# Transposing attention weights in 64-token halves, in turn from upper and lower rows into two banks

## The chip, the cores and the metric

One NeuronCore of a Trainium2 chip runs the whole program; the other cores are idle. The metric is device time in microseconds (us) of one execution, lower is better. The kernel before takes 581.49 us, the median of two executions (581.31 and 581.68).

## What is computed

Attention with a sliding window and sinks, followed by two feed-forward layers of two matrix products each, all in fp32:

```
scores = q @ k.T / sqrt(64)             # 2 batches, 8 heads, 768 tokens, head size 64
keep   = (column < n_sink) | (0 <= row - column < window)     # n_sink 4, window 128
a      = softmax(where(keep, scores, -1e9))
x      = (a @ v), heads side by side                          # 1536 tokens x 512
h = x @ w_in;  x = (h * clip(h + 3, 0, 6) / 6) @ w_out        # 512 -> 2048 -> 512
h = x @ w_in2; out = (h * sigmoid(1.702 * h)) @ w_out2        # 512 -> 2048 -> 512
```

## The kernel before

**Tiles.** There are 12 tiles of 128 tokens (`NTILE`). A tile's four pairs of heads are handled in two calls of `duo` (line 1122), so 24 duos of two pairs, four heads, each. One duo is: the scores on TensorE (PE), 24 small matmuls on 64x64 quarters of the array (L1152); for each of the four heads a masking with the row minimum on VectorE (DVE, L1167) and an exponential on ScalarE (ACT, L1175) into a tile `pexp` of 128 tokens by 196 keys, zero padded to 256; the inverse of the sums (DVE, L1183 and L1184); the scaling of `pexp` on DVE (L1194) or ACT (L1192); the transposes on PE (L1203), called "turns" here; and the copies of the transposed P from PSUM to the SBUF ring `pts` (ACT as L442, DVE as L444). After two duos `tile_values` (line 1215) multiplies P with V: 24 matmuls on 64 columns of the array (L1226, L1234). The result goes to SBUF as a high and a low part, `xy` (ACT L442, DVE L1253).

**Turns.** A turn takes one pair of heads: four transposes of 128x128, two heads by two chunks of keys, fill one PSUM bank of 512 columns, and one copy empties it into one `pts` tile. The transposed operand is the one that is loaded into the array (PEld), the identity is the one that is streamed.

**Feed-forward layers.** They run over blocks of 512 tokens and 16 slices of 128 hidden units: an "up" group is three matmuls of 128x512 per 128 inputs (L932), a "down" group three of 128x512 (L980), each on the whole array, with operands split in a high and a low part. The second layer of two of the three blocks is done later in another form (L616, L732). Weights are unpacked by DVE and ACT (L472 to L500).

**What sets the order.** Nothing is ordered by hand. `Plan` collects operations with costs per engine, dependences, buffers and due times, and `issue` emits them in the order of a greedy list schedule: each engine then runs its own list strictly in that order. So a change of costs, buffers or limits reorders the whole part in which attention and feed-forward work are mixed. `limit` (line 1295) decides which kind of work may take one of the eight PSUM banks: "s" scores, "t" turns, "v" values, "h" up, "y" down. The first block needs the first four tiles, so PE's list begins with attention alone (called the ramp here) and goes on with attention and feed-forward groups mixed until the twelfth tile; after it only feed-forward work is left.

## Time and profile before

| | us |
|---|---|
| median of two executions | 581.49 |
| the profiled execution | 582.17 |
| its span, first to last instruction | 580.4 |
| PE busy | 563.6 (97%) |
| DVE busy | 458.6 (79%) |
| ACT busy | 387.0 (67%) |
| POOL busy | 54.2 (9%) |

The profiled execution is 0.68 us above the median. Of its 582.17 us, 1.8 lie outside the span. Busy times of PE are modelled from starts, since matmuls overlap; pace is read from the distance of starts. PEld is the load of the array's stationary operand, which runs beside PE's matmuls. Most matmuls of plain fp32 data appear as two records each, the transposes as one.

### The profile page before, as it was taken

The numbers are of one execution on the slowest core, as the hardware profiler recorded it, in microseconds if no ns is written. First come the engines' busy times: TensorE is split into PE (matmuls) and PEld (weight loads), VectorE is DVE, ScalarE is ACT, GpSimd is POOL, SyncE is SP. The second block draws the span as 40 slices with busy tenths as digits, with TensorE's granted clock in tenths as the row PEclk, the third lists the DMA queues.
The fourth block names the chain that finished last, engine by engine and source line by source line (L and its number), as shares of the span: only waits on it lengthen the run. The fifth ranks groups of instructions, "written<-read, shape, count | busy, mean of one in ns | idle before, by whom it ended". The sixth has DMA issues, their size and how long they took to land.

```text
span 580.4 us, 11424 instructions
## 1 busy us (share of the span) xinstructions
PE 563.6 (97%) x4482; PEld 497.5 (86%) x4482; DVE 458.6 (79%) x958; ACT 387.0 (67%) x796; POOL 54.2 (9%) x62
## 2 busy tenths in 40 slices
PE   6889999999999999999999999999999999999996
PEld 6777887888878888888888888888888888999996
DVE  6699999999987666469999999984466665667784
ACT  6787768766755665456655678454478788768762
POOL 0000000000000000000000000000003344765000
PEclk8898999999999999999999999999999999999999
DMA  8973564234442000000444440420034567999512
GB/s 259 374 228 114 176 209 165 67 121 136 177 153 75 1 2 0 1 1 1 166 175 167 146 145 2 145 73 1 0 81 76 81 96 144 168 184 198 101 37 79
DMA packets 23468, 65.65 MB, mean 113 GB/s; under 512 B 2480, under 2 KB 10672, under 8 KB 19312
## 3 DMA queue, kind: packets, MB, share of 16 engines
q1 hardware_dynamic: 13360, 51.22, 26.4%
q0 software_dynamic: 10048, 13.63, 14.9%
q8 instruction: 37, 0.61, 0.4%
q14 instruction: 23, 0.19, 0.1%
HBM read 47.02 MB, written 3.15 MB: 86 GB/s over the span
## 4 chain that ended last, share of the span: by engine, by line
PE 79%; DVE 10%; ACT 4%; DMA 3%; issue 1%; DVEq 0%; SPq 0%; ACTq 0%
PE bank L932 24%; PE bank L980 23%; PE bank L732 13%; PE bank L616 13%; DMA stage<-in_w_dram 3%; PE bank L1203 2%; ACT pexp L1175 2%; DVE wf L500 2%; PE bank L1152 2%; DVE wf L493 1%; PE bank L1226 1%; PE bank L1234 1%; DVE pexp L1167 1%; DVE wg L565 1%; DVE wg L550 1%
## 5 line engine op out<-in xcount | busy, mean ns | idle before, releaser
L980 PE MATMUL bank<-wg 128*128 128x512 f32 x768 | 189.5, 381 | 0.8 <-ACT wg L442 0.8
L980 PEld LDWEIGHTS bank<-wg 128*128 128x128 f32 x768 | 143.7, 189 | 22.1 <-ACT wg L442 1.2
L932 PE MATMUL bank<-xy,w0h 128*128 128x512 f32 x512 | 155.9, 386 | 2.1 <-ACT xy L442 1.4
L932 PEld LDWEIGHTS bank<-xy,w0h 128*128 128x128 f32 x512 | 95.9, 190 | 16.4 <-issue 1.7
L932 PE MATMUL bank<-xy,w0l 128*128 128x512 f32 x256 | 97.7, 382 | 0.1
L680 POOL DMA_DIRECT2D wf<-wf x24 | 29.0, 1288 | 467.3 <-ACT wf L661 432.0
L442 ACT CAST wg<-wf 128x512 fp32r<-128x512 f32 x78 | 48.3, 620 | 30.8 <-PE bank L980 23.3
L944 ACT ACTIVATE u<-bank,three 128x512 f32<-128x512 f32 x48 | 32.8, 684 | 40.1 <-PE bank L932 39.9
L550 DVE TENSOR_TENSOR w0l<-wf,w0h 128x512 fp32r<-128x512 f32 x72 | 49.3, 685 | 12.2 <-ACT w0h L442 12.2
L932 PEld LDWEIGHTS bank<-xy,w0l 128*128 128x128 f32 x256 | 48.8, 191 | 7.5 <-DVE w0l L550 0.5
L550 DVE TENSOR_TENSOR wg<-wf,wg 128x512 fp32r<-128x512 f32 x64 | 43.9, 686 | 13.5 <-ACT wg L442 13.5
L949 DVE SCALAR_TENSOR_TENSOR u<-u,bank 128x512 f32<-128x512 f32 x48 | 32.7, 682 | 23.5 <-ACT u L944 23.5
L472 ACT ACTIVATE wf<-stage 128x1024 f32<-128x1024 f32 x32 | 38.0, 1187 | 18.5 <-DMA stage<-in_w_dram 17.7
L1175 ACT ACTIVATE pexp<-pexp,nb 128x196 f32<-128x196 f32 x96 | 42.9, 449 | 9.0 <-DVE nb L1167 8.8
L565 DVE TENSOR_TENSOR wg<-u,wg 128x512 fp32r<-128x512 f32 x64 | 43.9, 687 | 1.3 <-ACT wg L442 0.2
L442 ACT CAST wg<-u 128x512 fp32r<-128x512 f32 x59 | 36.6, 621 | 12.3 <-DVE u L949 12.3
L493 DVE SCALAR_TENSOR_TENSOR wf<-stage,wf 128x1024 int32<-128x1024 int32 x32 | 39.1, 1221 | 0.3
L500 DVE SCALAR_TENSOR_TENSOR wf<-stage,wf 128x1024 int32<-128x1024 int32 x32 | 39.0, 1220 | 0.3
L576 ACT ACTIVATE u<-bank 128x512 f32<-128x512 f32 x32 | 19.1, 596 | 29.0 <-PE bank L932 21.9
L616 PE MATMUL bank<-xy,w0h 128*128 128x512 f32 x128 | 38.1, 379 | 0.0
L442 ACT CAST w0h<-wf 128x512 fp32r<-128x512 f32 x60 | 36.7, 611 | 0.8 <-PE bank L616 0.5
L1203 PE MATMUL bank<-ident,pexp 128*128 128x128 f32 x192 | 29.3, 296 | 4.2 <-DVE pexp L1194 2.4
(188 smaller groups left out, 994.8 us busy)
## 6 DMA issues: line engine op xcount, KB each, us to landing
stage<-in_w_dram SPq DMA_DIRECT2D x32, 1024.0 KB, 4.9
wf<-wf POOLq DMA_DIRECT2D x24, 256.0 KB, 3.8
wf<-in_kq_dram SPq DMA_DIRECT2D x8, 520.0 KB, 11.3
vc<-in_vc_dram SPq DMA_DIRECT2D x12, 320.0 KB, 5.8
vb<-in_v_dram SPq DMA_DIRECT2D x10, 256.0 KB, 6.6
kept<-in_kq_dram SPq DMA_DIRECT2D x4, 520.0 KB, 11.0
aside<-wf SPq DMA_DIRECT2D x4, 256.0 KB, 3.0
aside<-wf POOLq DMA_DIRECT2D x4, 256.0 KB, 5.1
```

Source lines behind the costliest of these rows:

```text
L442: eng.copy(out, in_)
L472: lambda e: e.activation(w.tile.bitcast(F32), top.bitcast(F32), AF.Abs),
L493: lambda e: e.scalar_tensor_tensor(out=w.tile, in0=top, scalar=-0x40000000, in1=w.tile, op0=ALU.bitwise_and, op1=ALU.bitwise_or),
L500: lambda e: e.scalar_tensor_tensor(out=w.tile, in0=low, scalar=29, in1=w.tile, op0=ALU.logical_shift_right, op1=ALU.bitwise_or),
L550: lambda e: e.tensor_tensor(out=lo.tile[at], in0=of(), in1=hi.tile[at].bitcast(F32), op=ALU.subtract),
L565: lambda e: e.tensor_tensor(out=gl.tile, in0=parted(u.tile), in1=gh.tile.bitcast(F32), op=ALU.subtract),
L616: e.matmul(bank.tile, l, woven(r), start=(begin and j == 0 and k == 0), stop=(j == 1 and k == 2), skip_group_check=True,)
L732: e.matmul(to, l, woven(t), start=(begin and n == 0 and m == 0 and e4 % share == 0), stop=(n == pairs - 1 and m == 2), skip_group_check=True,)
L932: e.matmul(h.tile[:, :n], w, woven(x), start=(c == 0 and k == 0), stop=(c == NC - 1 and k == 2))
L980: e.matmul(yb.tile, l, woven(r), start=(begin and k == 0), stop=(end is not None and k == 2))
L1175: lambda e, n=n: e.activation(pes[n].tile[:, :W], pes[n].tile[:, :W], AF.Exp, bias=nbs[n].tile, scale=-1.0, accum_out=z.tile[:, n : n + 1],),
L1203: e.transpose(pt.tile[:, n * P : (n + 1) * P], pes[2 * a + j].tile[:, x * P : (x + 1) * P], ident)
```

## The change

P is transposed in halves of 64 tokens. A turn still takes one pair of heads, but its four transposes become eight: for each 128x128 piece first the upper 64 rows into one bank, then the lower 64 rows into a second bank. Both turns of a duo fill the same two banks (the second joins with `adds`), and only then two copies run, one per bank, each for both pairs of heads. The ring `pts` has 3 tiles of twice the size in place of 6. The planner's cost of a turn goes from 440 to 250, and `limit` keeps two banks free for turns ("spared") where up and down groups, and scores, would take them. The values read the same data from the larger tile.

```diff
@@ -52,7 +52,7 @@
 NU = 3
 NG = 2
 PX = 8
-NPT = 6
+NPT = 3
 
 APART = 8
 
@@ -1089,7 +1089,7 @@
 
     def plan_attention(plan, pool, due):
 
-        sizes = {"nb": (8, [P, 1], F32), "z": (3, [P, 4], F32), "pts": (NPT, [P, 4, P], F32)}
+        sizes = {"nb": (8, [P, 1], F32), "z": (3, [P, 4], F32), "pts": (NPT, [P, 8, P], F32)}
         for cls, (n, shape, dt) in sizes.items():
             plan.ring(cls, n, lambda k, cls=cls, shape=shape, dt=dt: pool.tile(shape, dt, name=cls, tag=f"{cls}{k}"))
         kept = [pool.tile([P, KQ], F32, name="kept", tag=f"kept{j}") for j in range(KEPT)]
@@ -1194,23 +1194,35 @@
                         e.tensor_scalar_mul(x, x, r)
 
                 plan.op([("DVE", 232), ("ACT", 350)], scale, when, reads=[z], writes=[pes[n]])
+            pt, pb = [Buf(cls="bank", kind="t") for _ in range(2)], Buf(cls="pts")
             for a in range(2):
-                pt, pb = Buf(cls="bank", kind="t"), Buf(cls="pts")
-
-                def turn(e, a=a, pt=pt):
+
+                def turn(e, a=a):
                     for n in range(4):
                         j, x = divmod(n, 2)
-                        e.transpose(
-                            pt.tile[:, n * P : (n + 1) * P], pes[2 * a + j].tile[:, x * P : (x + 1) * P], ident
-                        )
-
-                plan.op([("PE", 440)], turn, when, reads=pes[2 * a : 2 * a + 2], writes=[pt], chain="turn")
-                plan.op(
-                    [("ACT", 478), ("DVE", 602)],
-                    lambda e, pt=pt, pb=pb: copy(e, pb.tile, pt.tile.rearrange("p (n t) -> p n t", t=P)),
-                    when, reads=[pt], writes=[pb],
-                )
-                pts.append(pb)
+                        o = (4 * a + n) * HALF
+                        for c in range(2):
+                            rows = slice(c * HALF, (c + 1) * HALF)
+                            e.transpose(
+                                pt[c].tile[:, o : o + HALF], pes[2 * a + j].tile[rows, x * P : (x + 1) * P],
+                                ident[rows, rows],
+                            )
+
+                plan.op(
+                    [("PE", 250)], turn, when, reads=pes[2 * a : 2 * a + 2], chain="turn",
+                    **(dict(adds=pt) if a else dict(writes=pt)),
+                )
+            for c in range(2):
+
+                def take(e, c=c):
+                    at = pb.tile[:, :, c * HALF : (c + 1) * HALF]
+                    copy(e, at, pt[c].tile.rearrange("p (n t) -> p n t", t=HALF))
+
+                plan.op(
+                    [("ACT", 478), ("DVE", 602)], take, when, reads=[pt[c]],
+                    **(dict(adds=[pb]) if c else dict(writes=[pb])),
+                )
+            pts.append(pb)
 
         def tile_values(T, pts):
             i = tok[T][1]
@@ -1221,7 +1233,7 @@
 
             def values(e):
                 for hp in range(NPAIR):
-                    p = pts[hp].tile
+                    p = pts[hp // 2].tile[:, hp % 2 * 4 : hp % 2 * 4 + 4, :]
                     for j in range(2):
                         e.matmul(
                             av.tile[j * D : (j + 1) * D, hp * P : (hp + 1) * P],
@@ -1300,22 +1312,24 @@
                 used = [x.kind for x in slots if x is not None and (x.left or x in o.new)]
                 free = len(slots) - len(used)
                 h, v, t = (used.count(x) for x in "hvt")
+                spared = t or free > 2 or not plan.left["t"]
                 if b.kind == "h":
-                    return h < (H_BANKS if plan.left["s"] == 0 else 2 if "y" not in used else 1)
+                    return h < (H_BANKS if plan.left["s"] == 0 else 2 if "y" not in used else 1) and spared
                 if b.kind == "q":
                     return h + used.count("q") < (4 if "y" in used else 6)
                 if b.kind == "s":
                     mine = o.new.index(b)
                     if mine == 0 and used.count("s") > (0 if "y" in used else 2):
                         return False
-                    return free > (1 - mine if v or t else 2 - mine)
+                    return free > (1 if t else 2 if v else 3) - mine
                 if b.kind == "v":
                     return v == 0 or free > 2
                 if b.kind == "y":
-                    return used.count("s") < 4
+                    return used.count("s") < 4 and spared
                 if b.kind == "t":
 
-                    return t + sum(1 for x in plan.slots["pts"] if x is not None and x.left) < NPT
+                    mine = o.new.index(b)
+                    return mine or t // 2 + sum(1 for x in plan.slots["pts"] if x is not None and x.left) < NPT
                 return True
 
             plan.limit = limit
```

What the planner makes of it is seen in each engine's list. In PE's list, where the first up groups (L932) have begun, the kernel before has these rows: turns (L1203) of the fifth tile, its scores (L1152), twelve matmuls of down groups (L980), the last turns and the first rows of the values (L1226).

```order
L1203 MATMUL bank<-ident,pexp 128x128 x4
L932 MATMUL bank<-xy,w0h 128x512 x2
L932 MATMUL bank<-xy,w0l 128x512
L1203 MATMUL bank<-ident,pexp 128x128 x4
L1152 MATMUL bank<-wf 64x64 x8
L1152 MATMUL bank<-wf 64x68 x4
L1152 MATMUL bank<-wf 64x64 x8
L1152 MATMUL bank<-wf 64x68 x4
L980 MATMUL bank<-wg 128x512 x12
L1203 MATMUL bank<-ident,pexp 128x128 x8
L980 MATMUL bank<-wg 128x512 x3
L1226 MATMUL bank<-pts,vb_64 64x128 x2
```

The changed kernel has these at the same place; L1206 are its turns, eight transposes of 128x64 per pair of heads, L1238 and L1246 its values.

```order
L1206 MATMUL bank<-ident,pexp 128x64 x8
L932 MATMUL bank<-xy,w0h 128x512 x2
L932 MATMUL bank<-xy,w0l 128x512
L1206 MATMUL bank<-ident,pexp 128x64 x24
L1152 MATMUL bank<-wf 64x64 x8
L1152 MATMUL bank<-wf 64x68 x4
L1152 MATMUL bank<-wf 64x64 x8
L1152 MATMUL bank<-wf 64x68 x4
L1238 MATMUL bank<-pts,vb_64 64x128 x2
L1246 MATMUL bank<-pts,vc_66 64x64 x2
```

The last two turns moved up to the second, and the down groups moved behind the values, so turns, scores and values now stand next to each other.

Further on in PE's list, at the sixth tile, the kernel before has two turns between down groups and scores, and two between scores and down groups:

```order
L980 MATMUL bank<-wg 128x512 x12
L1203 MATMUL bank<-ident,pexp 128x128 x8
L1152 MATMUL bank<-wf 64x64 x8
L1152 MATMUL bank<-wf 64x68 x4
L1152 MATMUL bank<-wf 64x64 x8
L1152 MATMUL bank<-wf 64x68 x4
L1203 MATMUL bank<-ident,pexp 128x128 x8
L980 MATMUL bank<-wg 128x512 x6
```

The changed kernel at the seventh tile, where its pattern is plain:

```order
L980 MATMUL bank<-wg 128x512 x3
L1206 MATMUL bank<-ident,pexp 128x64 x16
L932 MATMUL bank<-xy,w0h 128x512 x2
L932 MATMUL bank<-xy,w0l 128x512
L932 MATMUL bank<-xy,w0h 128x512 x2
L932 MATMUL bank<-xy,w0l 128x512
L980 MATMUL bank<-wg 128x512 x9
L1206 MATMUL bank<-ident,pexp 128x64 x16
L980 MATMUL bank<-wg 128x512 x3
```

The two turns of a duo now mostly stand together, with groups on the whole array on both sides.

On ACT, ahead of the copy of the fourth tile's result (`xy`), for which the first up group waits, the kernel before has from the third tile's copy on:

```order
L442 CAST xy<-bank 128x4x128
L1192 ACTIVATE pexp<-pexp,z 128x196 x2
L1175 ACTIVATE pexp,z<-pexp,nb 128x196
L442 CAST w0h<-wf 128x512
L442 COPY pts<-bank 128x512
L1192 ACTIVATE pexp<-pexp,z 128x196 x2
L442 COPY pts<-bank 128x512
L442 CAST wg<-wf 128x2x256
L442 COPY pts<-bank 128x512
L1175 ACTIVATE pexp,z<-pexp,nb 128x196
L442 CAST xy<-bank 128x4x128
```

and the changed kernel:

```order
L442 CAST xy<-bank 128x4x128
L472 ACTIVATE wf<-stage_61 128x1024
L1192 ACTIVATE pexp<-pexp,z 128x196
L442 COPY pts<-bank 128x8x64
L442 CAST wg<-wf 128x2x256
L442 COPY pts<-bank 128x8x64 x3
L1175 ACTIVATE pexp,z<-pexp,nb 128x196 x3
L472 ACTIVATE wf<-stage_60 128x1024
L442 CAST xy<-bank 128x4x128
```

Four copies of P, three exponentials and two unpackings stand between the two `xy` copies now, where three copies, two exponentials and none stood before.

## Rows read from the trace of the kernel before

**Rows 1.** The page: granted TensorE clock in 40 slices of 14.5 us, in tenths.
```profile
PEclk8898999999999999999999999999999999999999
```

**Rows 2.** Stretches: from:to, length, busy time (and instructions) of each engine, clock, DMA share, GB/s.
```profile
5.00:43.10 38.10, 30.50 (x738) 26.50 (x738) 31.98 (x136) 30.68 (x103) 0.00 (x0) 0.87 0.91 306
...
50.00:80.00 30.00, 30.00 (x361) 25.76 (x360) 29.69 (x67) 20.04 (x45) 0.00 (x0) 1.00 0.44 143
80.00:210.00 130.00, 128.39 (x1337) 109.08 (x1337) 114.94 (x287) 88.91 (x212) 0.00 (x0) 1.00 0.33 111
```

**Rows 3.** Waits of PE from 50 to 210 us: total, times, longest.
```profile
PE bank L980 <- ACT wg L442: 0.8, 1, 0.8
PE bank L1203 <- ACT pts L442: 0.6, 1, 0.6
```

**Rows 4.** Timeline of PE: start, time, line, shapes, records (mixed part, full clock).
```profile
103.51 0.81 PE L980 MATMUL bank<-wg 128*128 128x512 f32 x3
104.16 0.60 PE L1203 MATMUL bank<-ident,pexp 128*128 128x128 f32 x4
104.52 0.89 PE L980 MATMUL bank<-wg 128*128 128x512 f32 x3
```

**Rows 5.** Timeline of PE in the ramp: turns between values and scores.
```profile
18.43 0.66 PE L1203 MATMUL bank<-ident,pexp 128*128 128x128 f32 x4
19.02 0.93 PE L1152 MATMUL bank<-wf 64*64 64x64 f32 x48
...
21.68 1.09 PE L1203 MATMUL bank<-ident,pexp 128*128 128x128 f32 x8
22.70 0.93 PE L1152 MATMUL bank<-wf 64*64 64x64 f32 x48
```

**Rows 6.** Timeline of PE: from the whole array to scores and back.
```profile
98.35 0.38 PE L932 MATMUL bank<-xy,w0l 128*128 128x512 f32 x1
98.66 0.93 PE L1152 MATMUL bank<-wf 64*64 64x64 f32 x48
99.52 0.48 PE L932 MATMUL bank<-xy,w0h 128*128 128x512 f32 x1
```

**Rows 7.** Timeline of PE inside scores: 24 records lie between these two starts.
```profile
111.81 0.29 PE L1152 MATMUL bank<-wf,kept 64*64 64x64 f32 x8
...
112.16 0.29 PE L1152 MATMUL bank<-wf,kept 64*64 64x64 f32 x8
```

**Rows 8.** Groups of loads (PEld) from 50 to 210 us: busy us, mean ns of one, idle.
```profile
L980 PEld LDWEIGHTS bank<-wg 128*128 128x128 f32 x258 | 47.5, 189 | 8.4 <-ACT wg L442 1.2 <-DVE wg L565 0.4 <-DVE wg L550 0.2
...
L1203 PEld LDWEIGHTS bank<-ident,pexp 128*128 128x128 f32 x128 | 14.8, 140 | 3.2 <-ACT pts L442 1.0 <-issue 0.2 <-DVE pexp L1194 0.2
...
L1152 PEld LDWEIGHTS bank<-kept 64*64 64x64 f32 x336 | 6.1, 134 | 2.0 <-issue 2.0
```

**Rows 9.** Timeline of loads: the first two loads of turns after values.
```profile
18.43 0.20 PEld L1203 LDWEIGHTS bank<-ident,pexp 128*128 128x128 f32 x2
```

**Rows 10.** The chain that ended last, pieces in the ramp: start, us, what.
```profile
13.60 1.44 PE bank L1203 x6
...
25.36 2.02 issue
...
28.90 2.76 PE bank L1203 x12
```

**Rows 11.** Groups of ACT in the ramp (5 to 43.1 us): busy us, mean ns of one, idle.
```profile
L1175 ACT ACTIVATE pexp<-pexp,nb 128x196 f32<-128x196 f32 x33 | 14.7, 449 | 3.4 <-DVE nb L1167 3.4
L442 ACT COPY pts<-bank 128x512 f32<-128x512 f32 x13 | 7.5, 579 | 1.8 <-PE bank L1203 1.8
...
L442 ACT CAST xy<-bank 128x512 fp32r<-128x512 f32 x4 | 2.3, 580 | 2.1 <-PE bank L1234 2.1
L472 ACT ACTIVATE wf<-stage 128x1024 f32<-128x1024 f32 x2 | 2.3, 1141 | 0.0
...
L442 ACT CAST w0h<-wf 128x512 fp32r<-128x512 f32 x2 | 1.2, 612 | 0.1
```

## The prediction

> **What bounds the kernel now.** I read the stretches first. From 50 to 210 us, where attention and feed-forward groups are mixed, PE is busy for 158.4 of 160 us [rows 2], and only two waits of it are named, 1.4 us together [rows 3]. DVE has 144.6 of the 160, in the first 30 us nearly all. So PE's list sets the end there, DVE stands close behind, and what PE saves or loses up to 210 us goes to the end one to one, since after it the same feed-forward groups follow in both kernels. In the ramp, 5 to 43.1 us, no engine is full: PE 30.5, DVE 32.0, ACT 30.7 of 38.1 us [rows 2]. There the chain of waits shows what ends last: it runs through PE with turns in it (1.44 us for six, 2.76 us for twelve transposes), and through a stop of 2.02 us that nothing shown released [rows 10]. The granted clock is below nine tenths of full in the first, second and fourth slice of 14.5 us, and at nine tenths or more in all others [rows 1].
>
> **The turns themselves.** A block of four transposes lasts 0.59 us from its start to the scores' start, one of eight 1.02 us [rows 5], so four cost 0.43 us: 0.109 each. Between down groups the cost is the same and nothing is added at the edges: three down matmuls take 0.65 us at 0.216 each, 103.51 + 0.65 is 104.16, where the turn starts; the next group starts at 104.52 but lasts 0.89 us, 0.08 longer than the 0.81 of the one before, so it really runs from 104.60, and the turn held PE for 0.44 us [rows 4].
>
> A 64-row transpose is not in this trace. The nearest thing is the scores: also two row halves in turn, also one bank for each half, also 64 streamed columns. Their 24 records between two starts take 0.35 us [rows 7]; they stand in sets of four, two row halves by two column halves, so a set takes 0.058 us. In it the halves run side by side. The new transposes have two to a set, with a load of 128 columns for 64. Is that load the limit? The loads of turns last 140 ns on average, those of scores, with half the columns, 134, those of down groups, with the same columns, 189 [rows 8]. And the second load of a turn starts 0.06 us after the first, when nothing runs ahead (two loads cover 0.20 us, one lasts 0.14) [rows 9]. So it fits in the set too, and I take 0.060 us for a pair of halves, 0.24 us for a turn. Bounds: 0.058 from the scores, and from above 0.218, two full transposes one after the other.
>
> The Trainium skill, "TensorE: Matmul & The Clock Gate", section "LDWEIGHTS (loading the stationary operand)", says that a load takes its columns divided by 1.2 GHz, whatever the rows, so 107 ns for 128 columns. By that rule a pair could not go below 0.107, a turn would stay at 0.43 us, and the sum below would be +2.9 us in the place of -3.1. The loads of turns contradict it here, at 0.06 us; no row shows a load of 64 rows by 128 columns.
>
> In the mixed part there are 32 turns, 128 transposes (the other 64 are in the ramp): 128 x 0.109 = 14.0 us before, 32 x 4 x 0.060 = 7.7 after, **-6.3 us**.
>
> **The edges.** This is what the diff hides. Leaving the whole array for another cut of it is not free: the last up matmul starts at 98.35, the next slot would be 98.57, the scores start at 98.66: 0.09 us. Coming back, the first up matmul lasts 0.48 us where 0.38 is usual, its load lies open: 0.10 [rows 6]. A turn between values and scores gives the same [rows 5]: its 0.59 is 0.06 of open load, 0.436 of transposes, and 0.095 before the scores begin. So a change of cut costs 0.095 plus the load of what follows: 0.10 for the whole array, 0.06 for turns, 0.05 for scores and values. Until now a turn used the whole array and cost no change beside feed-forward groups. Now it has its own cut. I counted the changes over PE's list from the first up group to the last values: before 41 (20 to the whole array, 21 to scores or values), after 64 (27, 20, and 17 to turns). That is 20 x 0.20 + 21 x 0.145 = 7.0 us against 27 x 0.20 + 20 x 0.145 + 17 x 0.155 = 10.9: **+3.9 us**. A turn alone between groups gets dearer (0.59 for 0.44), two are about even (0.83 for 0.87), four gain 0.44; the regrouping in the list, with turns next to scores, keeps this loss from being larger.
>
> That a row cut alone makes a change is not shown in this trace, all changes in it also cut the columns. From below its price is nothing. The Trainium skill, "TensorEngine Tiling (Array Packing)", section "Key Properties", says that a switch of the tiling mode drains the engine. The 0.09 us at the scores' start agrees for a cut that is there [rows 6], and I take the full price.
>
> **One set of scores** (24 matmuls, 12 sets of 0.058) stands ahead of the first up group now, where PE waits anyway: **-0.7 us**.
>
> **Copies, buffers, waits.** There are 48 copies of 128x512 before and after, 46 on ACT for 44. The new ones write runs of 64; the copies of `xy`, which write runs of 128, cost 580 ns against 579 [rows 11], so I add nothing. What changes is their time: both copies of a duo start only after its second turn, 1.16 us on ACT for the two, and the values stand behind them in PE's list. In the mixed part one to three groups of 0.65 us cover that at most places; at one tile four turns are followed by two groups, 1.3 us against four copies of 0.58, of which the first two start 0.5 us early. If the cover fails at all eight tiles by 0.5 us, it costs 4 us; I take nothing. DVE, the engine close behind, by the lists loses 6 of its 66 scalings and 2 of its 4 copies to ACT, so it leaves PE's gain room.
>
> **The ramp.** Before the fourth `xy` copy ACT has 2 exponentials, 2 copies and 1 unpacking more and 1 split copy less: 0.9 + 1.16 + 1.14 - 0.61 = +2.6 us, if nothing of it falls into ACT's idle 7 us. Against it, the 6.4 us of turns on the chain (five pieces, of which the first and the last are shown [rows 10]) go to about 0.55 of that: -2.9 us. Also the stop of 2.02 us may move or go, since PE has 192 matmuls more. I take **0**, between +2.6 and -2.9.
>
> **Sum.** -6.3 + 3.9 - 0.7 + 0 = -3.1 us. On the profiled execution's 582.17 us that is 579.1; this lies 0.68 above the median, so on the median 578.4 us, 0.5% less.
>
> **Rivals.**
> 1. *No change of cut by rows alone.* Then the 17 changes to turns (2.6 us) and the 15 from turns straight to feed-forward groups (3.0) fall away: -8.7, 572.8 us. For it: turns keep all 128 output columns. Against it: the scores, the only row cut in the trace, pay.
> 2. *The halves don't run side by side*, each takes its 0.055 in turn, or the load is the limit. Then a turn stays at 0.44, 14.0 in place of 7.7: +3.2 us, 584.7; with the ramp's upper end 587. For it: transposes may not share the array as products do. Against it: the sets of scores [rows 7] and the open load of a turn [rows 9]. The rule on loads of the Trainium skill, named above, would end in this case too, within 0.3 us.
> 3. *Other engines eat the gain*: values wait for copies that start later, or DVE, at 29.7 of 30 us from 50 to 80, becomes the bound. With 0.5 us at eight tiles: 582.4.
> 4. *Slower by over 2%: halves one after another with the load open*, 8 x (0.055 + 0.06) = 0.92 us a turn. In the mixed part 32 x 0.92 = 29.4 for 7.7, +21.7, and about +4 on the ramp's chain: 604. It decides from a turn of 0.55 us on ((593.1 - 578.4) / 48 = 0.31 above 0.24). Against it: the loads of scores go beside running matmuls.
>
> **How the numbers follow.** Forecast 52%, rival 1 12%, rival 2 17%, rival 3 14%, rival 4 5%. The range runs from rival 1 (572.5) to rival 2 near the ramp's upper end (586.5), which leaves out rival 4 and the tails; the forecast's own, with the ramp's two ends, is 575.5 to 581. About 2%, 11.6 us, is what counts here as a difference. No case but rival 4 comes above 593.1, and only rival 1 with the ramp's best end comes near 569.9: faster 0.02, same 0.93, slower 0.05.
>
> **What would show it.** In the timeline of the changed kernel: starts of the pairs of L1206 0.06 us apart (rival 2: 0.11, rival 4: 0.2); an up or down matmul after a turn 0.10 longer than usual and 0.09 open before a turn's first load (rival 1: neither); the first up group at 43 to 44 us within 2 us (the ramp); PE's waits from 50 to 210 us below 2 us (rival 3: 4 or more, named after copies or DVE). Last values some 3 us earlier than 210 us, with six more feed-forward matmuls ahead of them. If pairs go at 0.06 and the time is still not below 581, waits or the ramp have taken it.

## The result, and the profile after

588.42 us, the median of two executions (587.66 and 589.18), beside 581.49: a ratio of 1.0129, 95% interval 1.0109 to 1.0149. So the change costs 1.3%, inside the 2% band, but on the other side of no change from the forecast of 578.4 us and above its range. The profiled execution is the one of 587.66 us, with a span of 585.9, 5.5 longer than before.

First the turns. In the timeline of PE after (start, time, line, shapes, records), where feed-forward groups have begun:

```profile
51.60 0.38 PE L932 MATMUL bank<-xy,w0l 128*128 128x512 f32 x1
51.91 0.46 PE L1206 MATMUL bank<-ident,pexp 64*128 64x64 f32 x8
52.31 0.70 PE L932 MATMUL bank<-xy,w0h 128*128 128x512 f32 x2
52.84 0.38 PE L932 MATMUL bank<-xy,w0l 128*128 128x512 f32 x1
53.16 0.97 PE L1206 MATMUL bank<-ident,pexp 64*128 64x64 f32 x24
54.05 0.33 PE L1152 MATMUL bank<-wf 64*64 64x64 f32 x2
```

Eight halves hold PE from 51.91 to 52.31, 24 of them from 53.16 to 54.05: 16 more halves, eight pairs, cost 0.49 us, 0.061 a pair. That is the forecast's pace, and it answers [rows 5]. The up matmul ahead of the turn has its slot until 51.60 + 0.216 = 51.82, so 0.09 us are open before the turn; the two up matmuls behind it last 0.70 where 0.59 is usual, 0.11 of open load. From 51.82 to 52.31 + 0.11 the turn of one pair of heads costs 0.60 us. The prediction's prices (0.24 + two changes of cut) give 0.59, beside 0.44 for a whole turn before [rows 4].

The Trainium skill, "TensorEngine Tiling (Array Packing)", section "Key Properties", says that a switch of the tiling mode drains the engine; the 0.09 us agree, for a cut by rows alone too. The Trainium skill, "TensorE: Matmul & The Clock Gate", section "LDWEIGHTS (loading the stationary operand)", would give 107 ns for a load of 128 columns. Here the two loads of a pair start side by side and the next two follow after 61 ns, so the measurement decides against it for these transposes.

Then the granted clock (40 slices of 14.6 us), and the stretches of [rows 2] (from:to, length, busy time and instructions of PE, PEld, DVE, ACT, POOL, clock, DMA share, GB/s):

```profile
PEclk8778999999999999999999999999999999999999
5.00:43.10 38.10, 27.48 (x766) 24.80 (x766) 29.41 (x135) 30.34 (x102) 0.00 (x0) 0.77 0.89 302
50.00:80.00 30.00, 26.94 (x279) 22.36 (x279) 27.68 (x64) 20.46 (x46) 0.00 (x0) 0.94 0.44 148
80.00:210.00 130.00, 126.50 (x1436) 105.65 (x1433) 115.84 (x284) 87.65 (x209) 0.00 (x0) 1.00 0.35 115
```

In the ramp PE is busy for 27.48 us where it was 30.50, and its clock is 0.77 of full where it was 0.87. From 50 to 80 us PE was full at full clock and now has 3 us of holes; its clock of 0.94 there is one stretch at the lower clock, from 56.1 to 59.5 us, behind the longest of them. Who made the holes, PE's waits from 50 to 215 us say (total, times, longest):

```profile
PE bank L1152 <- ACT pts L442: 1.7, 1, 1.7
PE bank L980 <- ACT pts L442: 1.1, 1, 1.1
PE bank L980 <- DVE u L949: 0.7, 1, 0.7
PE bank L932 <- ACT pts L442: 0.7, 1, 0.7
PE bank L1206 <- ACT pts L442: 0.6, 1, 0.6
PE bank L1152 <- DVE nb L1167: 0.5, 1, 0.5
PE bank L932 <- DVE nb L1167: 0.5, 1, 0.5
```

With two smaller ones they are 6.4 us, 1.4 before [rows 3], and 4.1 of them are for ACT's copies of P. I count the program in two parts: the ramp, up to the start of the second up matmul (44.28 us before, 47.40 after: +3.1), and the mixed part, from there to the start of the 541st feed-forward matmul, which stands behind the last values in both (167.4 us before, 169.5 after: +2.1). From there on the distance stays at 5.2 to 5.3 us to the start of the last matmul; the span, with what follows that matmul, is 5.5 longer.

### The profile page after: what moved, and what is told of

Its sections match the earlier page's. It is cut to its first block, busy times and chain, and to the rows that moved or that the text cites. A ratio compares the mean times of both kernels' runs of the same rounds, so it can differ in the third digit from the quotient of the medians.

```text
span 585.9 us, 11822 instructions
## 1 busy us (share of the span) xinstructions
PE 561.5 (96%) x4674; PEld 494.4 (84%) x4674; DVE 457.1 (78%) x952; ACT 388.8 (66%) x802; POOL 54.1 (9%) x62
## 4 chain that ended last, share of the span: by engine, by line
PE 86%; DVE 7%; ACT 2%; issue 2%; DMA 1%; DVEq 0%; ACTq 0%
PE bank L980 27%; PE bank L932 25%; PE bank L732 13%; PE bank L616 12%; PE bank L1238 2%; PE bank L1152 2%; PE bank L1246 2%; PE bank L1206 2%; DVE pexp L1167 1%; DMA stage<-in_w_dram 1%; ACT pts L442 1%; DVE wf L500 1%; DVE w0l L550 1%; DVE wf L493 1%; ACT wf L472 1%
## 5 line engine op out<-in xcount | busy, mean ns | idle before, releaser
L980 PE MATMUL bank<-wg 128*128 128x512 f32 x768 | 188.4, 381 | 2.3 <-ACT pts L442 1.1
L980 PEld LDWEIGHTS bank<-wg 128*128 128x128 f32 x768 | 144.0, 189 | 24.4 <-ACT pts L442 1.3
L932 PE MATMUL bank<-xy,w0h 128*128 128x512 f32 x512 | 154.4, 383 | 1.3 <-ACT pts L442 0.7
L932 PEld LDWEIGHTS bank<-xy,w0h 128*128 128x128 f32 x512 | 95.5, 189 | 15.8 <-ACT pts L442 0.8
L932 PE MATMUL bank<-xy,w0l 128*128 128x512 f32 x256 | 97.2, 380 | 0.1
L680 POOL DMA_DIRECT2D wf<-wf x24 | 28.5, 1239 | 473.0 <-ACT wf L661 437.3
L442 ACT CAST wg<-wf 128x512 fp32r<-128x512 f32 x79 | 48.9, 618 | 32.3 <-PE bank L980 24.2
L932 PEld LDWEIGHTS bank<-xy,w0l 128*128 128x128 f32 x256 | 48.4, 189 | 7.4 <-DVE w0l L550 0.7
L1175 ACT ACTIVATE pexp<-pexp,nb 128x196 f32<-128x196 f32 x96 | 43.1, 453 | 10.7 <-DVE nb L1167 10.5
L565 DVE TENSOR_TENSOR wg<-u,wg 128x512 fp32r<-128x512 f32 x64 | 43.8, 685 | 1.5 <-ACT wg L442 0.6
L442 ACT CAST w0h<-wf 128x512 fp32r<-128x512 f32 x58 | 35.6, 613 | 0.9 <-DVE wf L500 0.5
L1167 DVE CUSTOM_DVE_ANT_0 pexp<-bank,mask 128x196 f32<-128x196 f32 x96 | 29.8, 354 | 1.7 <-PE bank L1206 1.2
```

Source lines behind the costliest of these rows:

```text
L442: eng.copy(out, in_)
L565: lambda e: e.tensor_tensor(out=gl.tile, in0=parted(u.tile), in1=gh.tile.bitcast(F32), op=ALU.subtract),
L932: e.matmul(h.tile[:, :n], w, woven(x), start=(c == 0 and k == 0), stop=(c == NC - 1 and k == 2))
L980: e.matmul(yb.tile, l, woven(r), start=(begin and k == 0), stop=(end is not None and k == 2))
L1167: lambda e, j=j, n=n, cols=cols: e.tensor_tensor_reduce(out=pes[n].tile[:, :W], in0=sc[j].tile[:, cols], in1=masks[kind], scale=-SCALE, sc ...
L1175: lambda e, n=n: e.activation(pes[n].tile[:, :W], pes[n].tile[:, :W], AF.Exp, bias=nbs[n].tile, scale=-1.0, accum_out=z.tile[:, n : n + 1],),
```

## The experiments

All kernels compute the whole result. Each was timed beside runs of the kernel before (medians of 580.6 to 581.7 us), so the ratios are to be compared. "Ramp" and "mixed" are the two parts above, "waits" the sum of PE's waits from 50 to 215 us, taken before rounding, and "low" the time at the lower of the two clocks within the ramp and within the mixed part, all in the one profiled execution, in us. Executions of one kernel differ by some us (full_by_pair 583.55 to 588.23), so what one profile alone shows of a part is less sure than a difference of medians. And 3.4 us at the lower clock cost PE some 1.7 us (an estimate: up matmuls stand 0.43 us apart there, 0.21 elsewhere), so mixed parts are to be compared only where their low time is the same. "Structure" is the rest of the change without the halves: two banks filled by both turns, then two copies, the planner's cost, limits and order.

| kernel | median | ratio, 95% interval | ramp | mixed | waits | low, ramp / mixed |
|---|---|---|---|---|---|---|
| before | 581.49 | | 44.3 | 167.4 | 1.4 | 10.2 / 3.4 |
| after | 588.42 | 1.0129 (1.0109 to 1.0149) | 47.4 | 169.5 | 6.4 | 20.5 / 3.4 |
| full_by_chunk | 585.29 | 1.0072 (1.0047 to 1.0096) | 45.7 | 169.1 | 4.1 | 10.2 / 3.4 |
| full_by_pair | 586.04 | 1.0082 (1.0054 to 1.0111) | 48.0 | 168.6 | 3.5 | 6.8 / 3.4 |
| copies_apart | 584.71 | 1.0056 (1.0034 to 1.0078) | 45.7 | 168.7 | 4.1 | 13.7 / 3.4 |
| turn_440 | 588.98 | 1.0135 (1.0108 to 1.0161) | 49.9 | 169.9 | 5.9 | 23.0 / 0.9 |
| ramp_full | 584.97 | 1.0057 (1.0038 to 1.0075) | 45.7 | 167.9 | 5.4 | 6.8 / 0.0 |
| late_full | 588.90 | 1.0131 (1.0105 to 1.0157) | 49.5 | 169.6 | 4.3 | 20.5 / 3.4 |
| apart_full | 583.98 | 1.0051 (1.0033 to 1.0069) | 44.0 | 168.8 | 2.2 | 3.4 / 3.4 |
| ramp_filled | 586.67 | 1.0111 (1.0082 to 1.0139) | 48.3 | 167.1 | 5.0 | 10.2 / 0.0 |
| before_filled | 582.30 | 1.0025 (0.9999 to 1.0050) | 44.5 | 168.4 | 3.7 | 10.2 / 0.0 |
| apart_filled | 581.44 | 0.9999 (0.9981 to 1.0017) | 44.6 | 168.7 | 4.4 | 6.8 / 3.4 |
| before_250 | 580.94 | 1.0005 (0.9989 to 1.0020) | 43.8 | 166.5 | 1.8 | 3.4 / 3.4 |
| before_spared | 583.06 | 1.0032 (1.0012 to 1.0051) | 44.9 | 168.6 | 1.6 | 3.4 / 3.4 |
| chunk_unspared | 584.85 | 1.0073 (1.0049 to 1.0097) | 46.1 | 167.8 | 4.0 | 6.8 / 0.0 |
| after_unspared | 587.34 | 1.0101 (1.0070 to 1.0132) | 48.5 | 167.2 | 5.4 | 20.5 / 0.0 |
| apart_full_unspared | 580.64 | 1.0003 (0.9987 to 1.0020) | 44.0 | 166.7 | 0.9 | 11.5 / 5.6 |
| unspared_ramp_full | 584.57 | 1.0057 (1.0038 to 1.0077) | 45.5 | 166.3 | 4.2 | 6.8 / 0.0 |
| first_halved | 585.02 | 1.0062 (1.0041 to 1.0083) | 47.8 | 168.8 | 3.6 | 13.7 / 3.4 |
| doubled | 608.32 | 1.0449 (1.0395 to 1.0503) | 72.2 | 166.7 | | 45.4 / 5.8 |

### Halves or structure

The changed kernel with whole transposes: the two banks now hold the two chunks of keys, both still filled by both turns. The order of the operations on PE is that of after.

```diff
-                        o = (4 * a + n) * HALF
-                        for c in range(2):
-                            rows = slice(c * HALF, (c + 1) * HALF)
-                            e.transpose(pt[c].tile[:, o : o + HALF], pes[2 * a + j].tile[rows, x * P : (x + 1) * P], ident[rows, rows])
+                        o = (2 * a + j) * P
+                        e.transpose(pt[x].tile[:, o : o + P], pes[2 * a + j].tile[:, x * P : (x + 1) * P], ident)
```

> The changed kernel with whole 128x128 transposes again: each turn puts its pieces of the first chunk of keys into one bank and those of the second chunk into the other, so both copies still wait for both turns of a duo. All lists of the engines are those of the changed kernel (588.4 us), only PE's transposes differ. Theory A, the halves are not what costs, but the late copies and the list built around them: turns rise by 6.3 us in the mixed part, 17 changes into turns and 15 from turns to feed-forward groups fall away (5.6 us), so 588 to 592 us. Theory B, the halves themselves cost (dear changes of the array's cut): back to 581 to 584 us.

585.29 us lies between the two: the halves cost some 3 us, the structure the other 4. So there are two causes. The next kernel gives each turn its own bank, in the same order, so that the first copy may start after the first turn (`pt[a].tile[:, n * P : ...]`):

> As full_by_chunk, and the same lists on every engine, but each turn fills a bank of its own, so the first copy of a duo can start after the first turn. Theory A1, the copies start too late because they wait for the second turn: 2 to 4 us below full_by_chunk, and PE's waits named after copies of P fall by as much. Theory A2, the order of the lists is what costs, whatever a copy waits for: within 1 us of full_by_chunk.

586.04 us, no faster than full_by_chunk: that the first copy waits for the second turn is not what costs here.

### The planner's part of the structure

In copies_apart the planner no longer puts the second copy of a duo behind the first; then 9 of the 48 copies go to DVE, in the place of 2. In turn_440 a turn has its old cost again.

```diff
-                plan.op(
+                o = plan.op(
                     [("ACT", 478), ("DVE", 602)], take, when, reads=[pt[c]],
                     **(dict(adds=[pb]) if c else dict(writes=[pb])),
                 )
+                o.deps = list(pt[c].writers)
```

> The changed kernel, but in the planner's dependences the second copy of a duo no longer follows the first (it wrote the same buffer with adds, so it was planned behind it). Halves, banks and costs stay; the lists change: 9 copies go to DVE where it was 2, and the 48 turns stand in 18 runs on PE for 23. Theory A (late copies): PE's waits for copies fall below 3 us and five runs fewer save 5 x 0.35 us of edges: 583 to 585 us. Theory B (halves cost by themselves): 586 to 588 us.

> The changed kernel with the planner's cost of a turn back at 440 for 250; what runs stays the same, the lists change. Theory A2 (the list was built on a turn that is too cheap, since 250 leaves out the changes of cut at its ends): 583 to 585 us. Theory A1 (late copies): the waits for copies stay, 587 to 589 us.

The tie between the copies costs 3.7 us with halves (1.0129 to 1.0056). The planner's cost of a turn is not the cause: 588.98 with 440. In the kernel before, with nothing else changed, it does nothing either, while the sparing of banks alone costs 1.9 us:

> The kernel before with one part of the change alone: the planner's cost of a turn 250 for 440, whole transposes, one bank and one copy per turn as before. Only the lists change (18 runs of turns on PE for 24). If the list built on a turn that is too cheap is what is left of the loss (some 4 us once the ramp's halves are whole again): 583 to 585 us. If banks and copies by two pairs are: 580.5 to 582 us.

> The kernel before with one part of the change alone: the rules that keep two banks free for turns (up and down groups, scores), turns, copies and costs as before. If these rules are what is left of the loss: 583 to 585 us, with more waits of PE for work behind turns. If not: 580.5 to 582 us.

### Halves in the ramp, halves later

`if T < 4` (ramp_full) or `if T >= 4` (late_full) ahead of the whole form above; the order on PE is that of after in both.

> The changed kernel with whole transposes (in the banks of full_by_chunk) in the first four tiles, halves in the other eight; all lists are those of the changed kernel. Between them lie 588.4 us (halves everywhere) and 585.3 us (whole everywhere). Theory C, the halves hurt in the ramp: they are sent out faster, PE runs into the end of its fetched instructions earlier and works less, so the clock stays low longer: all of the 3 us comes back, 585 us, first up group near 45.5 us. Theory D, the halves hurt in the mixed part by their edges: 588 us.

> The opposite: halves in the first four tiles, whole transposes in the other eight, lists as in the changed kernel. Theory C: 588 us, first up group near 47.4 us. Theory D: 585.3 us.

584.97 beside 588.90: in this order, what the halves cost arises in the ramp's four tiles, and after the ramp they are worth nothing that shows in the time (585.29 with whole transposes throughout). apart_full has the lists of copies_apart with whole transposes throughout:

> copies_apart (584.7 us; its 48 turns stand in 18 runs) with whole transposes in the banks of full_by_chunk, the lists those of copies_apart. It prices the halves alone in a list that has fewer runs. By the sum of the prediction: 7.7 us turns to 14.0 and 18 runs lose about 0.33 us of edges each, so +0.4 us in the mixed part: 585 us. If the ramp's effect (theory C) is there too: 582 to 583 us.

583.98 beside 584.71: in these lists halves throughout cost 0.7 us, or 0.05% by the ratios, within the intervals. So the 3 us of the halves appear only with the tie between the copies (1.0129 beside 1.0072), hardly without it (1.0056 beside 1.0051). Why is not shown; in copies_apart the ramp has 0.6 us of waits for copies of P where after has 2.7, and 13.7 us at the lower clock where after has 20.5.

Where the ramp's loss arises, PE's timelines of after and of ramp_full show, from the second tile's values on. After:

```profile
27.37 0.82 PE L1152 MATMUL bank<-wf 64*64 64x64 f32 x40 [2.59 <-issue]
28.12 0.44 PE L1238 MATMUL bank<-pts,vb 128*64 128x128 f32 x4
...
32.29 1.81 PE L1206 MATMUL bank<-ident,pexp 64*128 64x64 f32 x24 [0.41 <-ACT pexp L1192]
34.03 2.34 PE L1152 MATMUL bank<-wf 64*64 64x64 f32 x96
36.30 0.44 PE L1238 MATMUL bank<-pts,vb 128*64 128x128 f32 x4
...
42.35 0.67 PE L1238 MATMUL bank<-pts,vb 128*64 128x128 f32 x4 [1.48 <-ACT pts L442]
...
45.92 0.93 PE L1152 MATMUL bank<-wf 64*64 64x64 f32 x48
46.78 0.48 PE L932 MATMUL bank<-xy,w0h 128*128 128x512 f32 x1
```

ramp_full, the same operations:

```profile
27.63 0.39 PE L1152 MATMUL bank<-wf 64*64 64x64 f32 x9 [2.57 <-issue]
27.95 0.44 PE L1246 MATMUL bank<-pts,vb 128*64 128x128 f32 x4
...
31.02 1.79 PE L1205 MATMUL bank<-ident,pexp 128*128 128x128 f32 x12 [0.46 <-ACT pexp L1192]
32.74 1.65 PE L1152 MATMUL bank<-wf 64*64 64x64 f32 x96
34.31 0.44 PE L1246 MATMUL bank<-pts,vb 128*64 128x128 f32 x4
...
39.53 0.44 PE L1246 MATMUL bank<-pts,vb 128*64 128x128 f32 x4
40.87 0.45 PE L1254 MATMUL bank<-pts,vc 68*64 68x64 f32 x8 [0.90 <-ACT pts L442]
...
42.61 0.93 PE L1152 MATMUL bank<-wf 64*64 64x64 f32 x48
44.92 0.46 PE L932 MATMUL bank<-xy,w0h 128*128 128x512 f32 x1 [1.37 <-ACT xy L442]
```

Both kernels have the stop of 2.6 us that nothing shown released, and both start the second tile's values at 28.0 to 28.1. Then the one with halves falls behind: 96 scores take from 34.03 to 36.30, 2.27 us where the other takes 1.57, and 24 halves take as long as 12 whole transposes, 1.74 and 1.72. By the third tile's values 2.0 us are lost. From 28.8 to 35.6 us the windows say why (last three columns: clock, DMA share, GB/s), after, ramp_full and ramp_filled, in this order:

```profile
28.80:35.60 6.80, 6.39 (x124) 5.85 (x124) 3.69 (x19) 4.30 (x13) 0.00 (x0) 0.50 0.66 218
```

```profile
28.80:35.60 6.80, 6.34 (x178) 5.51 (x176) 4.96 (x21) 5.58 (x19) 0.00 (x0) 1.00 0.67 214
```

```profile
28.80:35.60 6.80, 6.24 (x162) 5.45 (x166) 5.32 (x20) 5.72 (x21) 0.00 (x0) 1.00 0.70 245
```

The clock is at its lower level, 1.2 GHz, through the whole stretch after, and at 2.4 with whole transposes. The fourth tile's values then wait 1.48 us for the last copies, which start behind both turns (0.90 in ramp_full), and go at the lower clock again: the scores behind them start 3.3 us later than in ramp_full (45.92 beside 42.61). In ramp_full PE then waits 1.37 us for the copy `xy`, so 1.9 us are left at the first up matmul.

One stretch of one execution proves little: before and before_filled have one list up to 41.8 us, and from 28.5 to 31.8 us the clock is 0.50 in the one and 1.00 in the other. But the sums agree over all kernels. With halves in the ramp's four tiles the ramp has 13.7 to 23.0 us at the lower clock in five kernels (10.2 in ramp_filled, see below), with whole transposes there 3.4 to 11.5 in twelve. The stops that nothing shown released add to the scatter: full_by_pair, with whole transposes, has two in its ramp, 1.33 and 3.42 us, and a ramp as long as with halves (48.0).

### Is it the work that PE lacks?

If PE's clock stays low because halves leave it less to do, more work should help. ramp_filled is after with two products of `ident` by `ident` (128x128, overwritten by the turns) ahead of the first turn of each of the ramp's eight duos; before_filled and apart_filled have eight of them ahead of the first up group, apart_filled with whole transposes in the ramp and the tie between copies taken out.

```diff
+                    if T < 4 and a == 0:
+                        for _ in range(2):
+                            e.matmul(pt[0].tile[:, :P], ident, ident, start=True, stop=True)
```

> The changed kernel with two more whole-array matmuls (identity by identity, 128 columns, into a bank that the turn overwrites) ahead of the first turn of each of the eight duos of the ramp: some 0.44 us of work and two changes of cut more for each, about 5 us of PE in all. Theory C with the clock as the cause: the half-clock time before 50 us shrinks from 20 us, and the first up group comes no later than 47.4 us in spite of the added work, 586 to 588.5 us. Without the clock as cause: up to 4 us later, 589 to 592 us.

> The kernel before with eight more whole-array matmuls (identity by identity, into the bank that the first up group overwrites) ahead of the first up group, where PE stands idle from 41.5 to 43.1 us; lists else as before. After that wait the clock is at half from 45.5 to 48.9 us while PE runs up groups, which costs 1.7 us (twelve matmuls of 512 columns take 0.43 for 0.21 us). Theory C (idle PE brings the clock down): that stretch goes, 579.3 to 580.3 us. Without it: 581.2 to 582 us.

> copies_apart with whole transposes in the first four tiles, halves in the other eight, and the eight more matmuls of before_filled. It puts together what helped: apart_full (584.0 us) less up to 1.7 us of half clock from 44.6 us on, halves as good as whole ones in the mixed part (18 runs): 582 to 583 us. If the rest of the loss were the halves' after all, 584 us or more.

In ramp_filled the stretch at the lower clock from 28.8 us is gone (the third window above), and its ramp has 10.2 us at the lower clock, half of what after has. With 16 more products the time is 1.75 us shorter, 586.67, but the intervals overlap. So more work goes with more clock; that the clock makes the lost time is not shown by this pair. The products themselves delay the ramp (48.3 for 47.4 us), the stop behind 27 us is shorter in this execution (1.35 us for 2.59), and of the 2.4 us that the mixed part gets shorter 1.7 are the stretch at the lower clock from 56.1 us, which it does not have. before_filled missed its forecast of 579.3 to 580.3. The lower clock that before has from 45.5 to 48.9 us (0.50) is gone in it (1.00), but its ramp is no shorter (44.5 for 44.3), and in the mixed part PE's waits are 3.7 us for 1.4, the longest for DVE:

```profile
55.14 0.46 PE L983 MATMUL bank<-wg 128*128 128x512 f32 x1
57.06 0.70 PE L983 MATMUL bank<-wg 128*128 128x512 f32 x2 [1.46 <-DVE wg L550]
```

What the clock gives this kernel, the waits take back. apart_filled is level with before, 0.9999, and 0.5% below apart_full with intervals that don't overlap. Two things differ between these, the eight products and the halves after the ramp; which of them gave it is not shown.

### The old limits

The three kernels give scores, up and down groups the limits of before, without the sparing of two banks for turns.

```diff
-                    return free > (1 if t else 2 if v else 3) - mine
+                    return free > (1 - mine if v or t else 2 - mine)
```

> The run with whole transposes and the copies by bank for two pairs (585.29 us), with the limits of the kernel before for scores, up and down groups: the two banks are no longer kept free for turns. Theory A, the sparing costs its 1.9 us here as it did alone in the kernel before: 583.4 us, first up group at 45 us or earlier, feed-forward matmuls 2 to 540 within 168 us. Theory B, the loss lies in filling two banks together and copying them only then, whoever keeps them free: 585 us or more. Theory C, the sparing is needed once a duo takes two banks at once, since without it turns wait for banks: 587 us or more, with waits of PE for a bank's reader.

> The changed kernel, with halves, with the limits of the kernel before for scores, up and down groups. Six of the 48 copies of P go to DVE now, in the place of two. Theory A, the sparing costs 1.9 us: 586.5 us. Theory B: 588 to 589 us. Theory C: 590 us or more. In all of them the halves in the first tiles still cost their 3 us, so the first up group starts at 46 us or later.

> The same engine lists as the changed kernel with the old limits, with whole transposes in the place of halves, everything else alike. If the halves cost their 3 us through the ramp in these lists too, this kernel takes 3 us less than the one with halves (583.5 us beside 586.5), with its first up group about 2 us earlier. If the cost of the halves hung on the lists that the sparing makes, the two are equal within 1 us.

One premise of these expectations was wrong: after_unspared has 2 of its copies on DVE and not 6, and apart_full_unspared, which also lacks the tie between copies, has another order than it. The kernel to set beside after_unspared is chunk_unspared, with the same order on PE: 587.34 for 584.85, the halves cost 2.5 us there too. With the tie in place the sparing costs nothing (chunk_unspared 1.0073, full_by_chunk 1.0072). Without the tie it is all that is left: apart_full with it 1.0051, apart_full_unspared without it 1.0003. So two banks filled together and copied for two pairs cost nothing by themselves; the planner's tie and its sparing cost 4 us, and with whole transposes taking away only one of them gives 0.2% at most.

### Which part of the ramp's halves

On the order of after_unspared: whole transposes in the first four tiles; halves in the first tile alone. On that of apart_full_unspared: ahead of each whole transpose in four tiles, a transpose of its upper half into the same columns, which it overwrites.

```diff
+                            if T < 4:
+                                e.transpose(pt[x].tile[:, o : o + HALF], pes[2 * a + j].tile[:HALF, x * P : (x + 1) * P], ident[:HALF, :HALF])
                             e.transpose(pt[x].tile[:, o : o + P], pes[2 * a + j].tile[:, x * P : (x + 1) * P], ident)
```

> The lists of the changed kernel with the old limits (copies of six on DVE), whole transposes in the first four tiles, halves in the eight after them. If the halves are worth what they gave in this list after the first up group (167.5 us from feed-forward matmul 2 to 540 with halves beside 169.4 with whole transposes), and the ramp stays as with whole transposes (first up group at 41.3 us): 580.64 less 1.8, 578.9 us, below the kernel before. Rival: the mixed part gives nothing and the time stays at 580.6 us; or the ramp's length moves by itself, then the first up group is away from 41.3 by more than 1 us.

> The same lists; halves in the first tile alone, whole transposes in the eleven after it. Theory S, the stop of the first tile sets the ramp: PE runs out of instructions after eleven halves, 2.0 to 2.5 us at about 11.6 us, the first tile's values start 1.4 us later than with whole transposes (14.9), the first up group comes at 45 us or later: 584 to 587 us. Theory T, the halves of all four tiles each take their part: first up group by 43.5 us, 580 to 582.5 us.

> The same lists with whole transposes everywhere; in the first four tiles each whole transpose has a transpose of its upper half ahead of it, into the same columns, which the whole one overwrites. So PE has as many transposes there as with halves, and more work than with either. Theory I, the number of instructions makes the stop: PE stops at about 11.4 us for 2 us with nothing shown as releaser, the first up group is at 45 us or later, 584 to 588 us. Theory W, the halves cost because PE has less work and its clock stays at half: with more work no stop, first up group at 41 to 43 us, 580.5 to 582.5 us.

The first two were set beside 580.64 us by the same wrong premise; their level is chunk_unspared's 584.85. unspared_ramp_full is 584.57: halves after the ramp are worth no more than 0.3 us by the medians here as well, though in the profiled executions the mixed part is 1.5 us shorter with them (166.3 for 167.8) at nearly the same waits (4.2 and 4.0). first_halved leaves its question open. Its profiled execution loses 1.7 us of ramp against chunk_unspared's (47.8 for 46.1), most of the 2.4 that after_unspared loses, so the first tile's halves would be the main part; but that execution, 587.30 us, is the longest of its five, and the median of 585.02 is level with chunk_unspared, which speaks against it.

doubled missed the times of both theories, and measured another thing. PE's timeline of it in the first tile:

```profile
11.07 0.33 PE L1210 MATMUL bank<-ident,pexp 128*128 128x128 f32 x1
11.33 0.28 PE L1206 MATMUL bank<-ident,pexp 64*128 64x64 f32 x1
11.53 0.33 PE L1210 MATMUL bank<-ident,pexp 128*128 128x128 f32 x1
11.79 0.27 PE L1206 MATMUL bank<-ident,pexp 64*128 64x64 f32 x1
11.99 0.33 PE L1210 MATMUL bank<-ident,pexp 128*128 128x128 f32 x1
```

A half and a whole transpose repeat every 0.46 us. Their work is 0.055 (half of a whole transpose, an estimate) + 0.109 = 0.164 us, so each of the two changes of cut costs 0.148 us; the prediction had 0.155 for a change to turns. 128 such changes, and a lower clock for 45.4 us, hide in the time what the number of instructions does, but the stop can still be seen. Further on in the tile:

```profile
13.18 0.37 PE L1206 MATMUL bank<-ident,pexp 64*128 64x64 f32 x1
13.78 0.47 PE L1210 MATMUL bank<-ident,pexp 128*128 128x128 f32 x1 [0.23 <-issue]
```

The stop stands ahead of the twelfth transpose, as with halves, and lasts only 0.23 us, since eleven transposes take until then here.

## Why the prediction was wrong

**The turns (-6.3 us): right.** 0.061 us a pair, forecast 0.060. Rivals 2 and 4 fall with it.

**The edges (+3.9 us): right in price.** 0.60 us for a turn alone, 0.59 worked out; 0.148 us a change in doubled. Rival 1, no change by rows alone, falls. Turns and edges together can be read from kernels with one order on PE, halves beside whole transposes: mixed part less waits is 169.5 - 6.4 = 163.1 beside 169.1 - 4.1 = 165.0 (after, full_by_chunk), 164.6 beside 166.6 (copies_apart, apart_full), 161.8 beside 163.8 (after_unspared, chunk_unspared); the low time in the mixed part is the same within each pair. So halves give PE 1.9 to 2.0 us in the mixed part. The two terms' -2.4 is not the number to set beside it, since it holds the change of order too. In one order it is 6.3 less the 13 changes from groups to turns and the 15 back (13 x 0.155 + 15 x 0.20 = 5.0): 1.3 us. (Rival 1 takes away 17 changes to turns, but four of them come from scores and would stay changes; its time is 0.6 us too low.) From before to after the mixed part less its waits goes from 167.4 - 1.4 = 166.0 to 163.1: -2.9 us, beside the forecast's -3.1 for turns, edges and the set of scores.

**"Copies, buffers, waits: I take nothing": this step failed.** In the same three comparisons the waits rise by 2.3, 1.9 and 1.3 us, so they take back most or all of what the halves give; and with whole transposes they are at 4.1 us in full_by_chunk for 1.4 before, 1.8 of them for copies of P, as the new order places scores and groups behind copies that aren't ready, the rest mostly for DVE. In all 6.4 - 1.4 = 5.0 us, and -2.9 + 5.0 is the +2.1 measured for the mixed part. The text had the price, 4 us if the cover fails at all eight tiles, and set it to nothing in the forecast because groups cover it "at most places". Rival 3 is what came about there: it priced the waits at 4 us, 582.4, and the mixed part alone makes 581.5 + 2.1 = 583.6. My list of the work that stands behind a copy looked at values alone; the longest wait is of scores, 1.7 us.

**"The ramp: 0", between +2.6 and -2.9: this step failed too.** It is +3.1 us: +1.4 by the structure (44.3 to 45.7 with whole transposes, full_by_chunk) and +1.7 by the halves (+1.7 and +2.4 in the two other pairs). The bound was made from ACT's list and from a chain with shorter turns; it had no term for the clock. In the chain of after the stops without a releaser stand in the first two tiles:

```profile
11.59 1.89 issue
...
24.78 2.59 issue
```

The first of them is new in the chain, between the 11th and the 12th half of the first tile; the prediction had allowed only that the one of 2.02 us [rows 10] "may move or go". And with shorter turns beside such stops PE was longer at the lower clock, 20.5 us for 10.2 in full_by_chunk, where the other operations take longer too (96 scores 2.27 us for 1.57). -2.9 for faster turns had the wrong sign.

**The account.** Of the profiled executions: ramp +1.4 (structure) and +1.7 (halves), mixed part +1.7 (structure: 167.4 to 169.1) and +0.4 (halves: gain 1.9, waits 2.3), 5.2 in all, for 5.2 at the 541st feed-forward matmul. By the medians the halves have 3.1 us of 6.9, the structure 3.8; that split holds for the order with the tie between the copies, since without it the halves cost 0.7 us by the medians.

**The signs that were named.** Pairs at 0.06, the longer matmul behind a turn and the open 0.09: as forecast. First up group (43 to 44 us within 2), PE's waits below 2 us, last values 3 us earlier than 210: all three missed, at 46.78 us, 6.4 us, and 6.6 us later (the first of them at 214.91 for 208.29). The last sentence of the forecast, that with pairs at 0.06 and no better time waits or the ramp have taken it, is what happened, both at once.

**What stays open.** How much of the ramp's 1.7 us comes from the first tile's new stop and how much from the clock behind it, what makes the stops, and why the tie between the copies makes the halves dear. Whether halves after the ramp bring their 2 us in the order of apart_full_unspared, where PE's waits are 0.9 us, was not tried. No version was found that is faster than the kernel before.

## What to carry over

A planner that packs the work anew answers a local saving with a new order: price the order's waits from the kernel's own lists (which work stands behind each later copy, on every line and not only its reader) before the saving is booked, and test a change of shape apart from the limits that came with it. Where an engine isn't full, work taken off it need be no gain, and here it went with more time at the lower clock; bound such a stretch with the lower clock from the rows. A smaller operation that uses another cut of the array pays two changes each time it stands alone, of 0.15 us in doubled and 0.18 between groups ((0.60 - 0.24) / 2).

## What was not expected of the hardware

- In the first tile PE does not go past its eleventh transpose before 13.4 us in any trace here, whole or half: the twelfth starts at 13.47 to 14.33 us in all twenty kernels. after resumes at 13.47 us (11 of 32 halves done), full_by_chunk at 13.66 (10 of 16 whole transposes done). The seven kernels with halves in the first tile all have a stop without a releaser ahead of the twelfth, of 1.89 to 2.27 us; in the twelve with whole transposes alone that wait is 0.13 us at most, and what else they wait there is named after other engines. Two rows of after, then one of full_by_chunk:

```profile
10.88 0.70 PE L1206 MATMUL bank<-ident,pexp 64*128 64x64 f32 x11 [2.13 <-DVE pexp L1194]
13.47 1.34 PE L1206 MATMUL bank<-ident,pexp 64*128 64x64 f32 x21 [1.89 <-issue]
```

```profile
13.66 1.54 PE L1204 MATMUL bank<-ident,pexp 128*128 128x128 f32 x6 [0.18 <-ACT pts L442]
```

  From 11 to 22 us the DMA engines of both are full (a share of 1.0), and instructions come over a DMA queue of their own (38 packets, 0.62 MB, in after). That the stop is a late fetch of instructions would fit, and isn't shown. Behind it 21 halves take 1.34 us and the values wait 1.22 more for the copies, where in full_by_chunk six whole transposes are left and the values wait 0.32.
- The lower clock comes and goes by stretches of several us in the ramp. In one execution each, the same stop of 2.6 us is followed by 6.8 us at 1.2 GHz with halves (after) and by full clock with whole transposes (ramp_full); over the ramp the lower clock takes 13.7 to 23.0 us with halves, 3.4 to 11.5 with whole transposes, and 10.2 with halves and 16 idle products added.
- Loads of 64 rows by 128 columns for two row halves start side by side, a pair every 0.061 us. That is the 0.06 us at which one load of a whole turn was seen, for two of half the rows.
